# Keys' features times values in a linear-attention kernel: two heads to a product, 64 columns held and 34 moving

## The chip, the cores and the metric

The kernel runs on one core of one Trainium2 chip. The metric is the device time in microseconds of one execution. The core's engines are TensorE (PE; its weight loads are shown as PEld), VectorE (DVE), ScalarE (ACT), GpSimd (POOL) and SyncE (SP); transfers are issued from queues and run on 16 DMA engines. TensorE writes its products to PSUM, eight banks of 128 partitions x 512 fp32. A product holds one operand (the "held" columns, at most 128, loaded as weights) and streams the other (the "moving" columns, at most 512) past it. TensorE's array can be split by columns, so that several products with few held columns run side by side, each in its own tile and to its own partitions of PSUM.

## The reference

With S = 2048 rows, D = 512, H = 32 heads of 16 and F = 1792, all fp32:

```
qkv   = x @ wqkv                                  # q, k, v: 32 heads of 16 columns
phi_q = [softmax(q_h w_phi_h), softmax(-q_h w_phi_h)]     # 32 features a head
phi_k = [softmax(k_h w_phi_h), softmax(-k_h w_phi_h)]
kv_h  = phi_k_h^T v_h       (32 x 16)             # z_h = sum over rows of phi_k_h
o_h   = (phi_q_h kv_h) / (phi_q_h z_h + 1e-6)
a     = o @ wo
b     = relu(x @ w1 + b1)^2 @ w2 + b2
g     = sigmoid(sum(x * gate_w))
out   = g * a + (1 - g) * b
```

The change concerns kv_h and z_h: for every head the product of 32 features and 16 values (with a column of ones for z_h: 17), summed over all 2048 rows.

## The kernel before

**The order of the work.** The kernel doesn't issue instructions directly. A planner (class Plan) collects every operation with its reads and writes, gives each a cost (`lengths`, line 202) and a due time, and plays the engines forward. What it starts first on an engine comes first in that engine's instruction stream, so the order on every queue, the DMA issues of SP among them, is set by those costs. All instructions are issued from one line, L363, so the profile's groups are told apart by their tiles. TensorE's work is divided into groups (`nc.product()`); the planner looks at the first five groups that are left (LOOK) and takes the first that can start at the earliest time, so a group whose operands are late can be overtaken by up to four others. For a product of less than 128 x 128 held elements the planner's cost is that of line 214: at least 0.0214 us, and 0.00027 us per moving column for held blocks other than 1,024 elements.

**The stages.** Rows are taken in four blocks of 512, in two pairs r = 0, 1. A first phase makes the hidden layer x @ w1 and the queries ("u" products) and the keys' features and the values ("v" products) by a scheme with seven half-size products p1 to p7 in place of eight; each is split into a high and a low part and computed as three 128x512 products (`mm3`). Results of the hidden layer and the queries go to DRAM and come back later. A second phase, one step t for each of 4 x 14 blocks of w2, multiplies the hidden layer by w2 ("down"), and in between makes the queries' features (`do_e`, `do_phi`), the numerators (`do_n`), and the product with wo (`attend`).

**The keys' side.** The v products for one group of rows give two chunks of 128 rows: the keys' logits in banks vA and vB, the values in banks vE and vB. The steps are in `v_step`:

- p2 and p4 end the logits of the two chunks and call `features`: `exps` (largest and smallest of each head by two TENSOR_REDUCE, one subtraction of 1024 elements that writes each head twice, two exponentials on ScalarE), `sums` (sum and reciprocal) and `scaled`. The result, 32 features a head for 32 heads in the order of the heads, lies in a buffer e or ez.
- p7 and p3 put the values of the two chunks into vext[1] (an add on VectorE) and vext[0] (a copy on ScalarE). In vext each head has 17 columns, the last of which is one (set once by a memset).

`kv_burst` (line 721) then multiplies. It has 32 heads x 2 chunks = 64 fp32 products, each with 128 rows, 32 held feature columns and 17 moving value columns. Four heads go side by side into the four 32-column tiles of the array, and their results into the four groups of 32 partitions of bank kv, eight blocks of 17 columns each:

```
h = 8 * (b // 2) + 2 * a + b % 2
nc.tensor.matmul(ps[32 * a:32 * a + 32, b * VW:(b + 1) * VW], phi[:, 32 * h:32 * h + 32],
                 ve[:, h * VW:(h + 1) * VW], ...)
```

An add on VectorE takes the bank's 136 columns into kvs. There are eight bursts in a run, between 88 and 274 us; each is one group for the planner.

After the last, `kv_done` (line 735) spreads z from kvs (a copy and a transpose into zb, which lies in vext[0]) and puts the kv blocks into kvb, block by block for the numerators' product. `do_phi` on GpSimd and VectorE waits for zb, and `do_n` (32x32 tiles, 512 moving columns) for kvb and for the last of do_phi's transposes.

`exps` is used in three places: by `features` (tags e and ez), by `queries` for the first block (with a buffer passed in as `into`), and by `do_e` (tags XA...). `row()` hands out five buffers of 512 columns in turn.

Of the kernel before, what the change touches and what calls it, by code (L numbers as in the profile page):

```python
# [10 lines left out]
AF = mybir.ActivationFunctionType  # L11
ALU = mybir.AluOpType
# [5 lines left out]
P = 128  # L18
S, D, H, DH, F = 2048, 512, 32, 16, 1792
# [5 lines left out]
NG = 8  # L25
VW = DH + 1
# [349 lines left out]
def tile_gated_mix(ctx: ExitStack, tc: tile.TileContext, xT, xn, wqT, wkT, wphi, wv, wo, w1, b1, w2, b2, gw, out):  # L376
    nc = Plan(tc.nc)
# [3 lines left out]
    st, raw, held, turns = {}, {}, {}, {}  # L381
# [3 lines left out]
    def buf(tag, n=512, bufs=1, dtype=F32):  # L385

        i = turns[tag] = turns.get(tag, -1) + 1
        return View(Buffer(sbuf, shadows[n], f"{tag}_{i % bufs}", n, dtype), shadows[n])

    banks = {t: psum.tile([P, 512], F32, tag=t, name=t) for t in ("uA", "uE", "uB0", "uB1", "vA", "vB", "vE", "kv")}  # L390
# [9 lines left out]
    row = lambda: buf("row", 512, 5)  # L400
# [7 lines left out]
    def mm3(o, a, b, sa, sb, first, last):  # L408
        (ah, al), (bh, bl) = a, b
        for i, (x, y) in enumerate(((ah, bh), (ah, bl), (al, bh))):  # L410
            nc.tensor.matmul(o, x[:, sa], y[:, sb], start=first and i == 0, stop=last and i == 2, skip_group_check=True)
# [8 lines left out]
    const = lambda name, *shape: sbuf.tile([P, *shape], F32, tag=name, name=name)  # L420
# [3 lines left out]
    gate, rest = (const(n, NB * NC) for n in ("gate", "rest"))  # L424
    kvb = const("kvb", NK, 2, 2 * DH)
    tc.nc.gpsimd.memset(kvb, 0.0)
    kvs = const("kvs", NG * VW)
    tc.nc.gpsimd.memset(kvs, 0.0)
    wkept = dram.tile([NPW, 3, 2, P, 512], F32, name="wkept")
    wkept4 = dram.tile([NPW, 2, P, 256], F32, name="wkept4")  # L430
# [2 lines left out]
    vext = [const(f"vext{i}", H * VW) for i in range(2)]  # L433
    heads = lambda v: v.rearrange("p (h v) -> p h v", v=VW)
# [105 lines left out]
    def queries(b, k, src):  # L540

        t = row()
        nc.vector.transpose(t, src)
        if b == ORDER_B[0]:
            if k % 2 == 0:
                st["e0", k // 2] = buf(("tb", "phiT")[k // 2], 4 * D)
            st["e", 0, k] = sums(exps(t, into=st["e0", k // 2][:, k % 2 * 2 * D:(k % 2 + 1) * 2 * D]), f"r{k}")
        else:
            nc.sync.dma_start(qkept[b, k], t)
# [111 lines left out]
    def vproduct(ps, v, p, first, last):  # L661
        xo, ko = PAIRS[p]
        s = slice(v[1] * P, (v[1] + 1) * P)
        nc.product()
        for kk in range(2):
            mm3(ps, st["X", xo, kk], st["K", ko, kk], s, ALL, first and kk == 0, last and kk == 1)

    def exps(ps, tag="e", into=None):
        pv = ps.rearrange("p (h f) -> p h f", f=DH)
        ends = small("ends", 2 * H).rearrange("p (h t) -> p h t", t=2)  # L670
        ef = buf(tag, 2 * D, 2 if tag == "e" else 1) if into is None else into
        e = ef.rearrange("p (h t f) -> p h t f", t=2, f=DH)
        for t, op in enumerate((ALU.max, ALU.min)):
            nc.vector.tensor_reduce(ends[:, :, t], pv, AX.X, op)
        nc.vector.tensor_tensor(e, pv.unsqueeze(2).to_broadcast([P, H, 2, DH]), ends.unsqueeze(3).to_broadcast([P, H, 2, DH]),
                                ALU.subtract)
        for t, scale in enumerate((1.0, -1.0)):
            nc.scalar.activation(e[:, :, t, :], e[:, :, t, :], AF.Exp, scale=scale)
        return ef.rearrange("p (h f) -> p h f", f=DH)
# [11 lines left out]
    def features(n, ps):  # L691
        e3, r = sums(exps(ps, "ez" if n % 3 == 2 else "e"))
        st["phi", n] = scaled(e3, r)

    def v_step(v, p):
        n = 8 * v[0] + 2 * v[1]
        each = lambda x: x.rearrange("p (h f) -> p h f", f=DH)
        if p == "p1":
            vproduct(banks["vA"], v, p, True, False)
            nc.scalar.activation(banks["vB"], banks["vA"], AF.Copy)  # L700
        elif p == "p2":
            vproduct(banks["vA"], v, p, False, True)
            features(n, banks["vA"])
        elif p == "p5":
            vproduct(banks["vE"], v, p, True, False)
            st["t5", v] = slot("Vt5")
            nc.scalar.activation(st["t5", v], banks["vE"], AF.Copy)
        elif p == "p6":
            vproduct(banks["vB"], v, p, False, False)
            nc.vector.tensor_tensor(banks["vE"], banks["vB"], st["t5", v], ALU.add)  # L710
        elif p == "p7":
            vproduct(banks["vB"], v, p, False, False)
            nc.vector.tensor_tensor(heads(vext[1])[:, :, :DH], each(banks["vB"]), each(st["t5", v]), ALU.add)
        elif p == "p3":
            vproduct(banks["vE"], v, p, False, True)
            nc.scalar.activation(heads(vext[0])[:, :, :DH], each(banks["vE"]), AF.Copy)
        else:
            vproduct(banks["vB"], v, p, False, True)
            features(n + 1, banks["vB"])

    def kv_burst(v):
        n = 8 * v[0] + 2 * v[1]
        ps = banks["kv"]
        nc.product()
        for m in range(2):
            phi, ve = st["phi", n + m], vext[m]
            for b in range(NG):
                for a in range(4):
                    h = 8 * (b // 2) + 2 * a + b % 2
                    nc.tensor.matmul(ps[32 * a:32 * a + 32, b * VW:(b + 1) * VW], phi[:, 32 * h:32 * h + 32],  # L730
                                     ve[:, h * VW:(h + 1) * VW], start=(m == 0 and b == 0), stop=(m == 1),
                                     skip_group_check=True)
        nc.vector.tensor_tensor(kvs, kvs, ps[:, :NG * VW], ALU.add)

    def kv_done():
        kv = kvs.rearrange("p (b v) -> p b v", v=VW)
        z = row()[:, :NG * 32]
        nc.vector.tensor_copy(z.rearrange("p (b f) -> p b f", f=32), kv[:, :, DH].unsqueeze(2).to_broadcast([P, NG, 32]))
        nc.vector.transpose(zb, z)
        kv = kvs.rearrange("p (k u v) -> p k u v", u=2, v=VW)  # L740
        for m in range(2):
            nc.vector.tensor_copy(kvb[:, m::2, :, DH * m:DH * (m + 1)], kv[:, m::2, :, :DH])

# [50 lines left out]
    def do_e(i, k):  # L794
        t = load(slot(("XS30h", "XS30l", "XS31h", "XS31l")[k]), qkept[ORDER_B[i], k])
        n = NK * i + k
        st["e", i, k] = sums(exps(t, E_PLACES[n % 4]))
# [156 lines left out]
    def run(seq):  # L954
        for u, p in seq:
            if p == "burst":
                kv_burst(u)
            else:
                (v_step if len(u) == 3 else u_step)(u, p)
# [30 lines left out]
    vs1 = v_stream([(1, m, "kv") for m in range(NC)], (0, NC - 1, "kv"))  # L990
    run(us1[:2] + merged(us1[2:len(us1) - 5], vs1) + us1[len(us1) - 5:])
    kv_burst((1, NC - 1, "kv"))


# [4 lines left out]
    when = lambda s, f, *a: steps.setdefault(s, []).append(lambda: f(*a))  # L999
    NT = NB * NF  # L1000
    when(1, kv_done)
    when(5, wo_ready)
    for i in range(NB):
# [8 lines left out]
    for t in range(NT):  # L1012
        for f in steps.get(t, ()):
            f()
        i, f = divmod(t, NF)
# [11 lines left out]
        if last:  # L1027
            ends = [bank() for j in range(2)]
# [7 lines left out]
        for c in range(NC):  # L1036
            n = ORDER_B[i] * NC + c
# [58 lines left out]
```

## Time and profile before

| what | us |
|---|---|
| median of 3 runs | 484.05 (483.94 to 484.32) |
| the profiled execution | 484.64 |
| its span, first to last instruction | 482.8 |
| PE busy | 477.6 |
| DVE busy | 398.3 |
| ACT busy | 245.6 |
| POOL busy | 190.3 |
| DMA | 107.84 MB, mean 223 GB/s |

The span is what the engines' rows cover; the time of the execution is 1.8 us longer. A row of a group reads: line, engine, operation, output<-input, held rows*columns for TensorE, shapes, count | busy us, mean ns of one | idle us before it and who ended it. fp32 products appear as two LDWEIGHTS and two MATMUL rows each; a product on split operands (`mm3`) as one of each per part. Matmuls are pipelined: one of 512 columns lasts 0.39 us in the rows while the next starts 0.23 us after it.

### The profile page before, as it was taken

To read this page: it belongs to the slowest core of one execution; us is meant where nothing else is said; L and a number is where in the kernel's file an instruction comes from. 1 tells how busy PE (TensorE), PEld (TensorE's weight loads), DVE (VectorE), ACT (ScalarE), POOL (GpSimd) and SP (SyncE) were. 2 spreads that over 40 slices of the span, in tenths; PEclk is the share of its full clock that TensorE was granted. 3 is DMA by queue.
4 is the path that set the end of the run, shared out by engine and by line. 5 is a ranking of instruction groups with operands and counts; after the bars stand their busy time and mean duration, and the time that the engine had idled before them with its cause. 6 is when DMAs were issued, how large, how long until landed. Compare 5 with 4: busy or idle time off the path is not lost.

```text
span 482.8 us, 9455 instructions
## 1 busy us (share of the span) xinstructions
PE 477.6 (99%) x3512; PEld 384.1 (80%) x3512; DVE 398.3 (82%) x555; ACT 245.6 (51%) x439; POOL 190.3 (39%) x186
## 2 busy tenths in 40 slices
PE   9999999999999999999999999999999999999997
PEld 4878888888878888888888888788878887888785
DVE  4996898979897848999888879899999999991313
ACT  5896989642688656436688822532254205312200
POOL 1020657842663203111022489386457628740000
PEclk9999999999999999999999999999999999999999
DMA  7999867875588788855799996536612673326302
GB/s 272 365 401 335 301 236 270 298 271 175 198 261 260 256 296 284 280 197 148 260 344 329 336 368 200 181 128 207 218 57 64 193 260 115 109 88 191 93 0 87
DMA packets 61421, 107.84 MB, mean 223 GB/s; under 512 B 6848, under 2 KB 11200, under 8 KB 61376
## 3 DMA queue, kind: packets, MB, share of 16 engines
q1 hardware_dynamic: 60768, 106.33, 64.8%
q10 hardware_dynamic: 576, 0.92, 0.8%
q8 instruction: 27, 0.44, 0.4%
q14 instruction: 18, 0.15, 0.1%
q0 software_dynamic: 32, 0.01, 0.0%
HBM read 62.14 MB, written 45.09 MB: 222 GB/s over the span
## 4 chain that ended last, share of the span: by engine, by line
PE 91%; DMA 3%; DVE 3%; ACT 1%; SPq 1%; issue 0%; DVEq 0%; ACTq 0%
PE uB L363 29%; PE uA L363 16%; PE uE L363 16%; PE vB L363 10%; PE vA L363 8%; PE vE L363 7%; PE kv L363 5%; DMA KT30h<-in_w 1%; DMA wkept<-O0l 1%; DMA hkept<-b2b 1%; SPq L363 1%; DVE tb L363 0%; DVE O1l L363 0%; DVE XS11l L363 0%; DVE KT31h L363 0%
## 5 line engine op out<-in xcount | busy, mean ns | idle before, releaser
L363 POOL TENSOR_TENSOR ez<-XA,vext 128x512 f32<-128x512 f32 x24 | 34.3, 1446 | 22.3 <-DVE XS21l L363 7.3
L363 PE MATMUL uA<-XA,O0h 128*128 128x512 f32 x128 | 39.5, 390 | 0.0
L363 ACT ACTIVATE row<-row 128x512 f32<-128x512 f32 x53 | 32.2, 623 | 0.3
L363 ACT ACTIVATE XA<-XA 128x512 f32<-128x512 f32 x24 | 14.1, 630 | 34.3 <-DVE XA L363 34.2
L363 POOL TENSOR_TENSOR row<-row,wo 128x512 fp32r<-128x512 f32 x8 | 10.4, 1295 | 50.7 <-ACT wo L363 40.7
L363 PEld LDWEIGHTS uA<-XA,O0h 128*128 128x128 f32 x128 | 23.9, 188 | 5.0
L363 ACT ACTIVATE O0h<-ring 128x512 fp32r<-128x512 f32 x17 | 10.7, 628 | 31.2 <-PE uB L363 15.8
L363 PE MATMUL uA<-XA,O0l 128*128 128x512 f32 x64 | 24.9, 389 | 0.0
L363 POOL TENSOR_TENSOR row<-row,b2b 128x512 fp32r<-128x512 f32 x10 | 13.0, 1299 | 27.8 <-DMA qkept<-row 16.5
L363 DVE TENSOR_REDUCE dz<-ez 128x64 f32<-128x1024 f32 x16 | 19.3, 1205 | 2.6 <-POOL ez L363 2.6
L363 PE MATMUL uB<-XA,O3h 128*128 128x512 f32 x64 | 19.8, 391 | 0.0
L363 ACT ACTIVATE O1h<-ring 128x512 fp32r<-128x512 f32 x17 | 10.7, 630 | 14.5 <-PE uB L363 11.6
L363 DVE TENSOR_TENSOR XA<-XA,w 128x1024 f32<-128x1024 f32 x12 | 17.8, 1480 | 0.0
L363 DVE TENSOR_REDUCE sm<-e 128x64 f32<-128x1024 f32 x11 | 13.4, 1217 | 5.0 <-ACT e L363 4.9
L363 DVE RECIPROCAL r<-sm 128x64 f32<-128x64 f32 x32 | 17.1, 538 | 0.2
L363 ACT ACTIVATE row<-b2b,rest 128x512 f32<-128x512 f32 x16 | 10.8, 715 | 10.6 <-DMA out<-row 7.7
L363 POOL TENSOR_TENSOR O1l<-ring,O1h 128x512 fp32r<-128x512 f32 x9 | 13.8, 1533 | 4.8 <-ACT O1h L363 4.8
L363 ACT ACTIVATE wo<-row 128x512 fp32r<-128x512 f32 x17 | 10.6, 625 | 9.7 <-DMA hkept<-wo 8.4
L363 DVE TENSOR_TENSOR e<-e,r 128x1024 f32<-128x1024 f32 x11 | 15.0, 1374 | 0.2
L363 DVE TENSOR_TENSOR uE<-uB,ol 128x512 f32<-128x512 f32 x16 | 11.1, 692 | 4.4 <-PE uB L363 4.4
L363 ACT ACTIVATE e<-e 128x512 f32<-128x512 f32 x22 | 13.0, 622 | 3.1 <-DVE e L363 3.0
L363 DVE TENSOR_REDUCE sm<-XA 128x64 f32<-128x1024 f32 x12 | 14.3, 1202 | 0.0
(934 smaller groups left out, 1753.6 us busy)
## 6 DMA issues: line engine op xcount, KB each, us to landing
hkept<-row SPq DMA_DIRECT2D x53, 256.0 KB, 4.2
ring<-hkept SPq DMA_DIRECT2D x24, 256.0 KB, 2.7
hkept<-b2b SPq DMA_DIRECT2D x16, 256.0 KB, 3.1
hkept<-wo SPq DMA_DIRECT2D x16, 256.0 KB, 3.8
xn<-in_xn SPq DMA_DIRECT2D x16, 256.0 KB, 4.6
O0h<-hkept SPq DMA_DIRECT2D x16, 256.0 KB, 3.7
O0l<-hkept SPq DMA_DIRECT2D x16, 256.0 KB, 3.9
O1h<-hkept SPq DMA_DIRECT2D x16, 256.0 KB, 3.8
```

The lines of the kernel that those rows point to most:

```text
L363: call(*map(real, op.args), **{k: real(a) for k, a in op.kw.items()})
```

## The change

Two neighbouring heads of a burst share one product: 64 columns of features are held, and the 2 x 17 value columns of both heads move. Of the 64 x 34 result, the two diagonal 32 x 17 blocks are the heads' own, and the other two (one head's features with the other's values) are not used. A burst has 32 fp32 products in place of 64; they go into two 64-column tiles, to partitions 0 to 63 and 64 to 127.

For that the two heads have to lie side by side. The keys' features are written with the even heads first and the odd heads behind them (the subtraction of `exps` is made in two halves, only for tags e and ez without `into`), and the values are put into vext in the same order (`paired`, `paired_out`). kvs and the add behind a burst have 8 x 34 = 272 columns in place of 136. kv_done first copies the own blocks out of kvs into a row buffer, with four copies on VectorE, one for each 32 partitions, and goes on from there.

```diff
-    kvs = const("kvs", NG * VW)
+    kvs = const("kvs", NG * 2 * VW)
...
+    def paired(x, f):
+
+        return x.rearrange("p (n u f) -> p u n f", u=2, f=f)
+
...
-        nc.vector.tensor_tensor(e, pv.unsqueeze(2).to_broadcast([P, H, 2, DH]), ends.unsqueeze(3).to_broadcast([P, H, 2, DH]),
-                                ALU.subtract)
+        for u in range(2) if into is None and tag[0] == "e" else (None,):
+            o, i, n = (slice(u * H // 2, (u + 1) * H // 2), slice(u, H, 2), H // 2) if u is not None else (slice(0, H), slice(0, H), H)
+            nc.vector.tensor_tensor(e[:, o], pv[:, i].unsqueeze(2).to_broadcast([P, n, 2, DH]),
+                                    ends[:, i].unsqueeze(3).to_broadcast([P, n, 2, DH]), ALU.subtract)
...
-        each = lambda x: x.rearrange("p (h f) -> p h f", f=DH)
+        each = lambda x: paired(x, DH)
+        paired_out = lambda x: x.rearrange("p (u n v) -> p u n v", u=2, v=VW)[:, :, :, :DH]
...
-            nc.vector.tensor_tensor(heads(vext[1])[:, :, :DH], each(banks["vB"]), each(st["t5", v]), ALU.add)
+            nc.vector.tensor_tensor(paired_out(vext[1]), each(banks["vB"]), each(st["t5", v]), ALU.add)
...
-            nc.scalar.activation(heads(vext[0])[:, :, :DH], each(banks["vE"]), AF.Copy)
+            nc.scalar.activation(paired_out(vext[0]), each(banks["vE"]), AF.Copy)
...
-                for a in range(4):
-                    h = 8 * (b // 2) + 2 * a + b % 2
-                    nc.tensor.matmul(ps[32 * a:32 * a + 32, b * VW:(b + 1) * VW], phi[:, 32 * h:32 * h + 32],
-                                     ve[:, h * VW:(h + 1) * VW], start=(m == 0 and b == 0), stop=(m == 1),
+                for a in (0, 2):
+                    h = H // 2 * (b % 2) + 4 * (b // 2) + a
+                    nc.tensor.matmul(ps[32 * a:32 * a + 64, b * 2 * VW:(b + 1) * 2 * VW], phi[:, 32 * h:32 * h + 64],
+                                     ve[:, h * VW:(h + 2) * VW], start=(m == 0 and b == 0), stop=(m == 1),
...
-        nc.vector.tensor_tensor(kvs, kvs, ps[:, :NG * VW], ALU.add)
+        nc.vector.tensor_tensor(kvs, kvs, ps[:, :NG * 2 * VW], ALU.add)
 
     def kv_done():
-        kv = kvs.rearrange("p (b v) -> p b v", v=VW)
+
+        own = row()[:, :NG * VW]
+        for a in range(4):
+            rows = slice(32 * a, 32 * a + 32)
+            nc.vector.tensor_copy(own[rows].rearrange("p (b v) -> p b v", v=VW),
+                                  kvs[rows].rearrange("p (b j v) -> p b j v", j=2, v=VW)[:, :, a % 2, :])
+        kv = own.rearrange("p (b v) -> p b v", v=VW)
...
-        kv = kvs.rearrange("p (k u v) -> p k u v", u=2, v=VW)
+        kv = own.rearrange("p (k u v) -> p k u v", u=2, v=VW)
```

## The prediction

> **What bounds the kernel now.** I read the page's head first, then its chain of waits, then the stages.
>
> ```profile
> span 482.8 us, 9455 instructions
> PE 477.6 (99%) x3512; PEld 384.1 (80%) x3512; DVE 398.3 (82%) x555; ACT 245.6 (51%) x439; POOL 190.3 (39%) x186
> PEclk9999999999999999999999999999999999999999
> PE 91%; DMA 3%; DVE 3%; ACT 1%; SPq 1%; issue 0%; DVEq 0%; ACTq 0%
> ```
>
> TensorE is busy 99% of the span at full granted clock and carries 91% of the chain, so time added to or taken from its stream should move the end about one for one; 482.8 - 477.6 = 5.2 us is all the idle time there is to win back elsewhere. The columns of the next view, stages of the time in which the eight bursts run, are the stretch's length, then each engine's busy time.
>
> ```profile
> 162.00:192.00 30.00, 30.00 (x256) 24.76 (x255) 21.05 (x33) 19.75 (x37) 5.36 (x5) 1.00 0.87 290
> 192.00:222.00 30.00, 30.00 (x256) 24.76 (x255) 29.34 (x41) 11.88 (x21) 4.13 (x5) 1.00 0.63 203
> ```
>
> TensorE has no gap in either. VectorE (third) has 9 us to spare in one and 0.7 in the other: the second cover to watch.
>
> Now one burst (kv_burst, line 721), in the chain and then in the timeline:
>
> ```profile
> 86.98 1.36 PE uB L363 x6
> 88.34 1.20 PE kv L363 x82
> 89.54 1.59 PE uB L363 x6
> ...
> 88.27 1.27 PE L363 MATMUL kv<-vext,e 128*32 128x17 f32 x128
> 89.47 0.30 PEld L363 LDWEIGHTS uB<-XA,O3h 128*128 128x128 f32 x2
> ```
>
> The burst takes 1.20 us of the chain, and the product behind it 1.59 instead of 1.36, so 1.43 together and 8 x 1.43 = 11.4 us in all: the most that any version of the burst could save. The 64 products of the code are 128 matmuls, because each fp32 product is two passes, each with its own weight load.
>
> **What paces a burst.** The next view counts the burst's matmuls (second item) and loads (third item) from just before its start to four moments.
>
> ```profile
> 88.26:88.32 0.06, 0.05 (x4) 0.05 (x8) 0.00 (x0) 0.00 (x0) 1.00 1.19 444
> 88.26:88.35 0.09, 0.08 (x8) 0.08 (x12) 0.00 (x0) 0.00 (x0) 1.00 1.09 410
> 88.26:88.70 0.44, 0.43 (x50) 0.43 (x52) 0.00 (x0) 0.00 (x0) 1.00 1.01 373
> 88.26:89.20 0.94, 0.93 (x110) 0.93 (x112) 0.00 (x0) 0.00 (x0) 1.00 1.03 375
> ```
>
> From 88.70 to 89.20 come 60 matmuls, one per 8.3 ns. Four column tiles take them in turn, so a tile gets one pass per 33 ns. Two things could set that. One is the tile: at the start, where the instructions were queued up already, four loads (one per tile) came in each 0.03 us, which is about the time of a 32-column load itself. The other is the supply of instructions: a product (two loads, two matmuls) every 17 ns is also what the fold shows, in sixteen 32x32 tiles:
>
> ```profile
> 39.71 0.29 PE L363 MATMUL vB<-KT41h,KT40h 32*32 32x128 f32 x1
> ...
> 39.83 0.29 PE L363 MATMUL vA<-KT41h,KT40h 32*32 32x128 f32 x1
> ```
>
> Between these two starts lie 7 steps (vB, vE, kv, vA, vB, vE, kv, vA), so 0.12 / 7 = 17 ns each. Today supply and tile agree within what these rows resolve. The change pulls them apart: half as many products to supply, but 64 columns to load per pass and two tiles in place of four.
>
> What a 64-column load costs is not in the trace; the two ends are. Columns are min/median/max ns in the first row and busy us, mean ns in the second:
>
> ```profile
> L363 PEld LDWEIGHTS kv<-vext,e x704: 106/109/113, 88.3 to 273.4; 128*32 128x32 f32 x176
> L363 PEld LDWEIGHTS uA<-XA,O0h 128*128 128x128 f32 x128 | 23.9, 188 | 5.0
> ...
> 477.96 0.19 PEld L363 LDWEIGHTS vA<-KT40h,O0l 128*128 128x128 f32 x1
> ...
> 478.92 0.19 PEld L363 LDWEIGHTS vB<-KT41l,O1h 128*128 128x128 f32 x1
> ```
>
> From 32 to 128 columns a load grows from 106 to 188 ns, 82 / 96 = 0.85 ns per column. That makes an occupancy of 27 ns for 32 columns (the 0.03 above) and 109 for 128. The latter shows behind the burst: two loads within 0.30 us, each lasting 0.19, so the second began 0.11 after the first. For 64 columns my estimate is 55 ns. The turn of a tile is longer than its load by 33 - 27 = 6 ns in the burst and, in the last stage (eight steps from 477.96 to 478.92, 120 ns each), by 11. So a 64-column tile turns in 55 + 6 to 55 + 11, 61 to 66 ns, or 55 if nothing is added; I take 60. The moving columns hide under it, as two passes of 512 columns in one tile of the numerators' product show:
>
> ```profile
> 306.19 0.59 PE L363 MATMUL vA<-XA,kvb 32*32 32x512 f32 x1
> ...
> 306.61 0.59 PE L363 MATMUL vA<-XA,kvb 32*32 32x512 f32 x1
> 306.81 0.61 PE L363 MATMUL vB<-XA,kvb 32*32 32x512 f32 x1
> ```
>
> They are 0.42 us apart, so 34 columns take some 28 ns.
>
> **The sum, part by part.**
>
> 1. *The bursts.* Per tile 64 / 2 = 32 passes, as before 128 / 4 = 32. Each costs 60 instead of 33 ns: 32 x 27 = 0.86 us per burst, 8 x 0.86 = **+6.9 us**. With 55 it is 8 x 32 x 22 = +5.6, with 66 it is +8.4. Nothing hides it, since TensorE has no gap there.
> 2. *The product behind a burst.* It pays 1.59 - 1.36 = 0.23 us today. Part of that is the change of tile form, which stays; part is that the burst left no instructions in store, and a burst paced by its tiles would leave some. Between 0 and 8 x -0.23 = -1.8; I take **-0.2**, nearer the first, because one 109 ns load after the change of form is in it anyway.
> 3. *VectorE during the bursts.* exps subtracts in two halves for the 16 keys' features, and kvs grows to 272 elements.
>
> ```profile
> L363 DVE TENSOR_TENSOR e<-vB,ends 128x1024 f32<-128x1024 f32 x6 | 7.3, 1215 | 0.1
> L363 DVE TENSOR_TENSOR vE<-vB,Vt 128x512 f32<-128x512 f32 x8 | 5.5, 691 | 1.5 <-PE vB L363 1.5
> L363 DVE TENSOR_TENSOR kvs<-kvs,kv x8: 234/282/297, 90.5 to 273.9; 128x136 f32<-128x136 f32 x8
> ```
>
>    Two halves cost 2 x 691 - 1215 = 0.17 us more, two such splits per burst 0.33; the wider kvs add costs 136 more elements at (1215 - 691) / 512 = 1.02 ns, 0.14. That is 0.47 us of VectorE per burst against 0.86 more of TensorE: 29.34 + 0.47 still fits into 30.86. The paired order of p7's add and p3's copy moves the same 512 elements; I cost it at nothing under the same cover. But the planner (line 214) prices a small product at 0.0214 us whatever its columns, so it plans a burst 32 x 0.0214 = 0.68 us shorter, while I expect 0.86 longer. Behind each burst VectorE's written-out order then stands up to 1.5 us too early, and whatever is queued there behind an add that waits for TensorE waits with it. If that ate the cover in the tight stage, TensorE would wait up to about 1 us, once or twice: 0 to +2, I take **+0.3**, near nothing, since in the other stage 9 us are free. A re-made order may also save: at most a part of the 5.2 us of idle; I take nothing.
> 4. *kv_done.* Four copies of the own blocks come between the last kvs add and all that follows.
>
> ```profile
> 273.90 0.28 DVE L363 TENSOR_TENSOR kvs<-kvs,kv 128x136 f32<-128x136 f32 x1
> 274.21 0.29 DVE L363 COPY row<-kvs 128x256 f32<-128x256 f32 x1
> 274.42 0.29 DVE L363 COPY kvb<-kvs 128x64 f32<-128x64 f32 x2
> 275.21 3.00 POOL L363 TENSOR_TENSOR ez<-tb,vext 128x512 f32<-128x512 f32 x2 [3.53 <-DVE vext L363]
> 305.24 1.25 DVE L363 STREAM_TRANSPOSE XA<-phiT 128x1024 f32<-128x1024 f32 x1
> ...
> L428 POOL MEMSET kvs<- x1: 230/230/230, 2.2 to 2.2; 128x136 f32 x1
> ...
> POOL 1020657842663203111022489386457628740000
> ```
>
>    A copy of 136 elements lies between the 64 and the 256 of these rows; two short ones took 0.29 together, so one is 0.15 to 0.29 and four 0.6 to 1.2 us; with 0.14 for the wider add, zb is about 1 us later. GpSimd has been idle 3.53 us for zb at that point, and the chain from it ends in the transpose that lands at 306.49, in the middle of the numerators' product (do_n), which already lost 0.2 us to it (306.61 to 306.81). So this delay has little cover of its own; what hides it is that the planner may put up to four other products ahead of do_n. Between 0 and +1.2; I take **+0.3**. On VectorE the splits of the w2 and wo weights are queued behind the copies; they are due later and nothing else waits. No DMA is issued that was not before, one row slot more is turned over, and the longer memset of kvs (0.23 us today, at 2.2 us) lies in the first slice of the span, where GpSimd is a tenth busy.
>
> The Trainium skill ("VectorE: DVE Perf Modes", section "Two Vector instructions with no wait between them") has an instruction held until all earlier ones are done when it starts in another quadrant than the one before. The four copies start at partitions 0, 32, 64 and 96, so by that rule they would not overlap at all and the upper end of their bounds would hold; the sum would be 0.3 higher at most. No run here shows such copies.
>
> Sum: 6.9 - 0.2 + 0.3 + 0.3 = +7.3 us. The profiled execution took 484.64 us in all (1.8 around its span), which gives 491.9; it lies 0.6 above the median of the three, 484.05, on which I put the same +7.3: **491.3 us**.
>
> **Rivals.**
>
> *A turn costs the same whatever the columns.* Then a tile's 33 ns is a fixed price per pass, 32 passes cost 32 x 33 = 1.06 us as before, and only the +0.6 of steps 3 and 4 is left: 484.6, no change. For it: today's turn can be read as a floor. Against: loads of 32 and 128 columns differ by 82 ns. The Trainium skill ("TensorE: Matmul & The Clock Gate", section "Wait — 56ns, not 53.3ns?") has such a floor of about 25 ns between starts of small matmuls; by that figure, per tile, a burst would cost 0.80 us and the kernel would be some 2 us faster. The trace has 8.3 ns between starts, so a floor could only hold within one tile. 9%.
>
> *The supply of instructions alone paces the burst*, and it becomes faster. A product every 17 ns needs 32 x 17 = 0.54 us, 0.52 less than 1.06: 8 x -0.52 = -4.2, plus 0.6, gives 480.4. For it: the 17 ns in two quite different tile forms. Against: it decides only if a tile of 64 columns turns in 17 ns, as two tiles share the supply, and at the start of a burst, with the queue full, a tile of 32 columns took 28 to 33. 8%.
>
> *The two tiles don't run side by side* (or the form isn't taken as two tiles). 64 passes in a row at 60 ns are 3.84 us, 2.78 more than now, 8 x 2.78 = +22: 506. Against it: the four tiles of today plainly overlap. 3%.
>
> *VectorE becomes the bound behind the bursts*: the upper ends of steps 3 and 4, 2.0 + 1.2 instead of 0.6, so 491.3 + 2.6 = 493.9. For it: 29.34 of 30; against: most stages have room. 6%.
>
> **Chances and range.** The forecast has 74%. About 0.2%, 1 us, is what can be told from no change. Slower: 74 + 3 + 6 = 83%, less 1 for surprises: 82; same 9; faster 9. The forecast's own range, with 55 to 66 ns and the other bounds, is 488 to 494.5. Both rivals without a loss hold 17%, so the range reaches down to the no-change one, 484.0 to 494.5; outside are the supply rival, the tiles in a row and some 5% of the rest.
>
> **What would show it.** In the new profile the burst's matmuls read 128*64 with 34 moving, 64 to a burst, and a load lasts about 133 ns (106 + 32 x 0.85). Right: a burst's piece of the chain near 2.0 us and one matmul per 30 ns. Wrong: pieces of 1.1 (fixed turn) or 0.6 (supply). Step 4 is right if do_n starts with a wait under 0.5 us; step 3 if no gaps appear between the bursts.

## The result, and the profile after

| | before | changed |
|---|---|---|
| median, us | 484.0 (483.84 to 484.32) | 491.47 (491.12 to 492.09) |
| ratio | | 1.0152, 95% interval 1.0139 to 1.0164 |
| span of the profiled execution, us | 482.8 | 490.0 |
| TensorE instructions (MATMUL) | 3512 | 3000 |

The change removes 512 matmuls and as many weight loads, and the kernel is 7.5 us (1.5%) slower. The head of the page and the chain of waits of the changed kernel:

```profile
span 490.0 us, 8458 instructions
PE 484.5 (99%) x3000; PEld 389.8 (80%) x3000; DVE 393.6 (80%) x572; ACT 246.3 (50%) x439; POOL 197.5 (40%) x189
...
PEclk9999999999999999999999999999999999999999
...
PE 92%; DVE 3%; DMA 2%; issue 1%; ACT 1%; SPq 1%; DVEq 0%
```

TensorE still bounds it, at full granted clock, and its busy time has grown by 6.9 us, nearly all of the 7.2 that the span has. The burst that was shown of before now stands in the chain like this (start, length, engine, tile, count):

```profile
87.36 1.36 PE uB L363 x6
88.72 1.99 PE kv L363 x64
90.71 1.58 PE uB L363 x6
```

1.99 us in place of 1.20: 0.79 more, and 8 x 0.79 = 6.3 us. The product behind it takes 1.58, as it did (1.59). What is inside a burst, by tile (min/median/max ns) and by cumulative counts from just before its start (second item matmuls, third loads):

```profile
L363 PEld LDWEIGHTS kv<-vext,e x352: 132/138/139, 88.6 to 280.0; 128*64 128x64 f32 x176
L363 PE MATMUL kv<-vext,e x352: 223/224/246, 88.7 to 280.0; 128*64 128x34 f32 x176
...
88.64:89.14 0.50, 0.49 (x17) 0.49 (x18) 0.00 (x0) 0.00 (x0) 1.00 0.63 139
88.64:90.14 1.50, 1.49 (x52) 1.49 (x52) 0.00 (x0) 0.00 (x0) 1.00 0.86 281
```

By these counts 35 matmuls in 1.00 us are one per 28.6 ns. From the first of the burst's 64 matmuls to the last, 63 steps in 1.84 us, it is 29.1, so each of the two tiles turns in about 58 ns, where each of the four turned in 33. A load lasts 132 ns at the least, 26 more than one of 32 columns.

The rest of the loss shows in the numerators' first product. The first row is its first matmul, the second the first matmul of the product behind it, in the kernel before; then the same of the changed kernel, with the transpose it waits for:

```profile
305.73 0.61 PE L363 MATMUL vA<-XA,kvb 32*32 32x512 f32 x1
...
308.04 0.50 PE L363 MATMUL uA<-KT40h,O0h 128*128 128x512 f32 x1
```

```profile
314.40 0.61 PE L363 MATMUL vA<-XA,kvb 32*32 32x512 f32 x1
...
315.24 1.25 DVE L363 STREAM_TRANSPOSE XA<-phiT 128x1024 f32<-128x1024 f32 x1
...
317.57 0.50 PE L363 MATMUL uB<-KT40h,O0h 128*128 128x512 f32 x1
```

Before, it held TensorE for 308.04 - 305.73 = 2.31 us. Now it begins at 314.40, the transpose lands at 316.49, and the next product starts at 317.57: 3.17 us, 0.86 more. 6.3 + 0.86 is the whole 7.2 of the span; single waits elsewhere came and went and balance. The kernel before has one of 0.49 us at 144 that the changed one hasn't (0.72 us from one matmul's start to the next, where 0.23 is usual). One that came stands before the last burst, 0.46 us by the starts of the matmuls (0.69 from 275.91 to 276.60):

```profile
276.60 0.73 PE L363 MATMUL uB<-XA,O3h 128*128 128x512 f32 x2 [0.30 <-DVE row L363]
```

The add on VectorE that ends this wait (275.86 to 276.54) is queued behind a reduction of the keys' features, which had itself been held up 0.62 us by ScalarE.

### The profile page after: what moved, and what is told of

Same layout as the page of the kernel before. It is cut to its first block, busy times and chain, and to the rows that moved or that the text cites. A ratio compares the mean times of both kernels' runs of the same rounds, so it can differ in the third digit from the quotient of the medians.

```text
span 490.0 us, 8458 instructions
## 1 busy us (share of the span) xinstructions
PE 484.5 (99%) x3000; PEld 389.8 (80%) x3000; DVE 393.6 (80%) x572; ACT 246.3 (50%) x439; POOL 197.5 (40%) x189
## 4 chain that ended last, share of the span: by engine, by line
PE 92%; DVE 3%; DMA 2%; issue 1%; ACT 1%; SPq 1%; DVEq 0%
PE uB L363 29%; PE uE L363 16%; PE uA L363 16%; PE vB L363 10%; PE vA L363 8%; PE vE L363 7%; PE kv L363 6%; DMA KT30h<-in_w 1%; DMA wkept<-O0l 1%; SPq L363 1%; DVE ends L363 0%; DVE e L363 0%; DVE tb L363 0%; DVE O1l L363 0%; DVE row L363 0%
## 5 line engine op out<-in xcount | busy, mean ns | idle before, releaser
L363 POOL TENSOR_TENSOR ez<-XA,vext 128x512 f32<-128x512 f32 x24 | 35.3, 1492 | 14.8 <-DVE dz L363 7.6
L363 POOL TENSOR_TENSOR row<-row,wo 128x512 fp32r<-128x512 f32 x10 | 14.5, 1450 | 37.8 <-ACT wo L363 25.8
L363 ACT ACTIVATE XA<-XA 128x512 f32<-128x512 f32 x24 | 13.9, 633 | 22.5 <-DVE XA L363 22.5
L363 POOL TENSOR_TENSOR O0l<-ring,O0h 128x512 fp32r<-128x512 f32 x10 | 13.9, 1388 | 11.0 <-ACT O0h L363 11.0
L363 POOL TENSOR_TENSOR dz<-dz,r 128x64 f32<-128x64 f32 x16 | 10.2, 640 | 13.5 <-DVE r L363 9.6
L363 DVE TENSOR_TENSOR XA<-XA,w 128x1024 f32<-128x1024 f32 x12 | 15.3, 1274 | 0.0
L363 DVE TENSOR_TENSOR row<-uB,ol 128x512 f32<-128x512 f32 x17 | 11.6, 685 | 4.5 <-PE uB L363 3.6
```

The costliest lines, as they stand in the source:

```text
L363: call(*map(real, op.args), **{k: real(a) for k, a in op.kw.items()})
```

## The experiments

The theory was that the number of held columns sets the turn of a tile, because the loads pace a burst, and that the remaining microsecond comes from kv_done's copies and from the planner's price of a product. The medians of the kernel before that these runs are compared with were 484.17 to 484.3; differences from it in us are worked out from the ratios.

**34 moving, 32 held.** Only the moving side of the change, in the kernel before (vext gets 17 columns of ones behind the last head):

```diff
-ps[32 * a:32 * a + 32, b * VW:(b + 1) * VW], phi[:, 32 * h:32 * h + 32], ve[:, h * VW:(h + 1) * VW]
+ps[32 * a:32 * a + 32, b * 2 * VW:(b + 1) * 2 * VW], phi[:, 32 * h:32 * h + 32], ve[:, h * VW:(h + 2) * VW]
```

> The kernel before, with each product of a burst moving 34 value columns (its head's and the next one's) while it still holds 32; only the own 17 columns of each result are added into kvs. Theory (the columns held set the tile's turn): a burst keeps its pace of one matmul per 8.3 ns, its piece of the chain stays at 1.2 us, and the time is 484.0 to 484.5. Rival (the columns moved set it): a tile's turn goes from 33 to about 58 ns, a burst costs 0.8 us more, and the time is about 490.3.

484.18 us, ratio 0.9998 (0.9988 to 1.0009). The burst in its chain, and its matmuls:

```profile
88.16 1.24 PE kv L363 x116
89.40 1.58 PE uB L363 x6
...
L363 PE MATMUL kv<-vext,e x704: 192/197/219, 88.1 to 273.2; 128*32 128x34 f32 x176
```

Each matmul lasts 9 ns longer (192 for 183 at the least), and 128 of them take 1.24 us in place of 1.20. Twice the moving columns cost next to nothing: the second head's values are free, and the rival falls.

**64 held, 17 moving.** Only the held side, in the changed kernel:

```diff
-ps[32 * a:32 * a + 64, b * 2 * VW:(b + 1) * 2 * VW], phi[:, 32 * h:32 * h + 64], ve[:, h * VW:(h + 2) * VW]
+ps[32 * a:32 * a + 64, b * VW:(b + 1) * VW], phi[:, 32 * h:32 * h + 64], ve[:, h * VW:(h + 1) * VW]
```

> The changed kernel, with each product holding 64 feature columns but moving 17 value columns, those of the first of its two heads; kvs has 136 columns and kv_done reads it without the four copies, as before. The second head of each pair gets the first one's values, so its own block is left out. Theory (columns held): a tile's turn stays at 58.5 ns, the last matmul of a burst starts 1.84 us after the first, and the time is 8 x 0.79 = 6.3 us above before: 490.0 to 490.7. Rival (columns moved): a turn of about 33 ns, 484.0 to 484.5. Rival (supply of instructions, a product per 17 ns): about 480.

490.93 us, 1.0136 (1.0116 to 1.0155), 6.6 us above before (5.6 to 7.5).

```profile
88.12 1.98 PE kv L363 x64
90.10 1.59 PE uB L363 x6
```

The whole cost of the burst is there with half of the moving columns. The two runs together say that the held columns set the time.

**48 held, 17 moving** in the same 64-column tile. As the run before, with `phi[:, 32 * h:32 * h + 48]` to `ps[32 * a:32 * a + 48, ...]`.

> As the run with 64 held and 17 moving columns, but with 48 feature columns held in each product (half of the second head's features are left out too). If the turn of a tile grows with the columns held, it is 48 x 0.85 + 4 = 45 ns: the last matmul of a burst starts 1.41 us after the first, 8 x 0.32 = 2.6 us above before and some 0.3 for the rest, 486.5 to 488.2. If it is set by the tile's width of 64 whatever is held in it, the turn stays at 58.5 and the time at 490.5 to 491.5.

487.21 us, 1.0057 (1.0042 to 1.0072), +2.8.

```profile
L363 PEld LDWEIGHTS kv<-vext,e x352: 119/125/125, 87.5 to 275.9; 128*48 128x48 f32 x176
...
87.50:87.80 0.30, 0.29 (x13) 0.29 (x14) 0.00 (x0) 0.00 (x0) 1.00 0.20 7
87.50:88.70 1.20, 1.19 (x53) 1.20 (x54) 0.00 (x0) 0.00 (x0) 1.00 0.52 97
...
87.58 1.55 PE kv L363 x64
```

40 matmuls in 0.90 us, 22.5 ns each, make a turn of 45 ns in two tiles, as expected: not the width of the tile but the columns loaded into it count. The loads last 106, 119, 132 and 188 ns at 32, 48, 64 and 128 columns, 13 ns for each 16, or 0.81 to 0.88 ns a column. By the Trainium skill ("TensorE: Matmul & The Clock Gate", section "LDWEIGHTS (loading the stationary operand)") a load takes the number of its columns divided by 1.2 ns, whatever the rows. The trace agrees with the 0.83 ns a column of this in the differences alone: the durations are some 80 ns longer (106 ns at 32 columns, where an estimate by the page's figure is 27). The rows count for little here too: loads of 32 columns by 32 rows last 101 to 104 ns, by 128 rows 106 to 113.

**16 held, 17 moving.** Is there more to win on the other side? The kernel before, with half the features left out:

```diff
-ps[32 * a:32 * a + 32, b * VW:(b + 1) * VW], phi[:, 32 * h:32 * h + 32],
+ps[32 * a:32 * a + 16, b * VW:(b + 1) * VW], phi[:, 32 * h:32 * h + 16],
```

> The kernel before with only the first 16 of each head's 32 features held (the products for the softmax of the negated logits are left out, 64 products a burst as before). If the columns held alone set the pace, a tile's turn falls to about 14 + 4 = 18 ns and the last matmul of a burst starts 0.6 us after the first: 484 - 8 x 0.5 = 480. If the supply of instructions, a product per 17 ns, is a second bound that happens to lie at the same place, only the first 32 matmuls, which were queued up, come faster, the rest keep 8.3 ns, and the time is 483.5 to 484.3.

483.92 us, 0.9997 (0.9988 to 1.0006): nothing to win.

```profile
88.37:88.57 0.20, 0.19 (x28) 0.19 (x32) 0.00 (x0) 0.00 (x0) 1.00 0.94 338
88.37:88.77 0.40, 0.39 (x49) 0.39 (x51) 0.00 (x0) 0.00 (x0) 1.00 1.03 389
88.37:89.27 0.90, 0.89 (x109) 0.89 (x111) 0.00 (x0) 0.00 (x0) 1.00 0.99 371
```

From 88.77 to 89.27 come 60 matmuls, the same 8.3 ns each as with 32 columns. So there is a second bound that doesn't move with the columns, at two loads and two matmuls per 17 ns. The reading that fits is the supply of instructions, because only the first 33 matmuls, whose instructions could be stored up while the product before them ran, come faster: here 25 ns from one turn of a tile to the next (28 matmuls in the first 0.19 us), with 32 columns held 31.7, and behind them 33.3 in both. So 33 ns is not a fixed price of a pass, and with 32 held columns the two bounds lie nearly together, the supply a little above the loads. The 25 ns are not the 18 ns of the load either; whether a floor per tile (the Trainium skill's page above, section "Wait — 56ns, not 53.3ns?", has about 25 ns between starts of small matmuls) or the start of one instruction after the other holds them, these rows can't tell.

**The layout alone.** The changed order of features and values, with the old bursts, the old kvs and no copies:

```diff
-                for a in (0, 2):
+                for a in range(4):
...
-ps[32 * a:32 * a + 64, b * 2 * VW:(b + 1) * 2 * VW], phi[:, 32 * h:32 * h + 64], ve[:, h * VW:(h + 2) * VW]
+ps[32 * a:32 * a + 32, b * VW:(b + 1) * VW], phi[:, 32 * h:32 * h + 32], ve[:, h * VW:(h + 1) * VW]
```

> The changed layout alone: features written with even heads first in two halves, values in the same order, but bursts of 64 products with 32 columns held and 17 moving, kvs of 136 columns, kv_done without the copies. Theory: the extra VectorE work (16 x 0.17 = 2.7 us) is hidden behind TensorE, 484.0 within 0.5. Rival (VectorE bounds the tight stages): some of the 2.7 us appears, 485 to 486.7.

485.51 us, 1.0029 (1.0015 to 1.0043): +1.4 (0.7 to 2.1; the medians differ by 1.2). So the loss is the rival's in size; whether VectorE's work or the plan makes it, this run doesn't say. Which part of the layout it is was tried next.

**The layout alone, with one subtraction.** As that run, but the keys' subtraction is one instruction again, with a destination of four dimensions (`e` as "n u t f", read from a buffer in the order "u n t f").

```diff
-for u in range(2) ...: nc.vector.tensor_tensor(e[:, o], pv[:, i]..., ends[:, i]..., ALU.subtract)
+o4 = ef.rearrange("p (u n t f) -> p n u t f", u=2, t=2, f=DH)
+nc.vector.tensor_tensor(o4, i4, n4, ALU.subtract)
```

> The layout alone once more, but with the keys' subtraction as one instruction of 1024 elements that writes even heads first and odd heads behind them. If the 1.2 to 1.4 us of the layout come from the second VectorE instruction of each split (16 x 0.17 us with little cover), they go: 484.0 to 484.6. If they come from the other order of the values or of the plan, they stay: 485.0 to 486.0.

484.19 us, 1.0001 (0.9992 to 1.001): the loss is gone. The instruction by tile, split and unsplit:

```profile
L363 DVE TENSOR_TENSOR e<-vB,ends x12: 651/678/691, 77.5 to 267.5; 128x512 f32<-128x512 f32 x12
```

```profile
L363 DVE TENSOR_TENSOR e<-vB,ends x6: 1186/1221/1226, 77.4 to 265.8; 128x1024 f32<-128x1024 f32 x6
```

2 x 678 - 1221 = 0.135 us for each of the 16, 2.2 us of VectorE, of which 1.4 came through to the end, with bursts of 1.20 us. Taking it away settles that it is the split or the plan that comes with it. The plan does change: with the split GpSimd has 195 instructions and 206.6 us of work, without it 186 and 191.7, as before (186 and 190.3). Which of the two it is, and at which place the time is lost, stays open: the one profile of the split layout (a span of 483.2, from one of its faster executions) has no wait of that size.

**The copies alone.** The kernel before, with the four copies ahead of kv_done:

```diff
+        own = row()[:, :NG * VW]
+        for a in range(4):
+            rows = slice(32 * a, 32 * a + 32)
+            nc.vector.tensor_copy(own[rows]..., kvs[rows]...)
+        kv = own.rearrange("p (b v) -> p b v", v=VW)
```

> The kernel before, with the four copies of 32 partitions x 136 elements ahead of everything else in kv_done, and nothing else changed. Theory (the copies delay zb, and with it the chain that ends in the first numerators' product): that product takes up to 0.9 us longer than its 2.6 us, and the time is 484.5 to 485.0. Rival (other products go ahead of it): 484.0 within 0.3, and the 0.86 us that this product takes longer in the changed kernel comes from something else.

484.79 us, 1.0008 (0.9999 to 1.0018): +0.4, which the interval doesn't tell surely from nothing. The trace does show the delay at that place:

```profile
307.14 0.61 PE L363 MATMUL vA<-XA,kvb 32*32 32x512 f32 x1
...
310.19 0.50 PE L363 MATMUL uB<-KT40h,O0h 128*128 128x512 f32 x1
...
273.95 0.93 DVE L363 COPY row<-kvs 32x136 f32<-32x136 f32 x4
275.24 1.39 DVE L363 COPY kvb<-row 128x64 f32<-128x64 f32 x2
276.56 0.43 DVE L363 STREAM_TRANSPOSE vext<-row 128x256 f32<-128x256 f32 x1
...
275.14 1.34 POOL L363 TENSOR_TENSOR KB221l<-KT40l,KB221h 128x512 fp32r<-128x512 f32 x1 [8.31 <-ACT KB221h L363]
```

The numerators' product takes 310.19 - 307.14 = 3.05 us, 0.74 more than before (2.31, not the 2.6 that the expectation has), close to the 0.86 of the changed kernel. In the run with 64 held and 17 moving columns, which has the long bursts but not the copies, it takes 2.31 (from 312.65 to 314.96), as before. So with these plans the copies bring the delay, whether all of it reaches the end or only half.

**The planner told.** The changed kernel with one price changed:

```diff
+            if rows * cols == 64 * P:
+                return 0.25, 0.0693
             if rows * cols < P * P:
```

> The changed kernel with one number of the planner different: a product with 64 columns held costs 0.0693 us (32 of them 2.2 us, what a burst costs in the changed kernel's trace) in place of 0.0214. Theory (part of the loss beyond the bursts is a plan that takes them for 1.5 us shorter than they are): the 0.46 us wait before the last burst and some of the 0.86 us in the first numerators' product go, 490.3 to 491.0. Rival (the price only renames the order, the waits are those of the longer chain): within 0.4 of the changed kernel, 491.1 to 491.9. Under both the bursts keep their +6.3.

490.06 us, 1.0121 (1.0107 to 1.0135), 1.4 us faster than the changed kernel. Its bursts are the same; its first numerators' product isn't delayed any more, though the copies are still there, and the wait before the last burst is gone:

```profile
313.06 1.25 DVE L365 STREAM_TRANSPOSE XA<-phiT 128x1024 f32<-128x1024 f32 x1
...
313.43 0.61 PE L365 MATMUL vA<-XA,kvb 32*32 32x512 f32 x1
...
315.73 0.50 PE L365 MATMUL uB<-KT40h,O0h 128*128 128x512 f32 x1
```

2.30 us, as before the change. The copies delay zb here as much as in the changed kernel (it is ready 3.4 us after the last kvs add begins in both, 1.2 before the change), so the copies alone don't make the loss: it takes an order that doesn't put enough in front of the numerators. What is left, 5.9 us (5.2 to 6.5), is the bursts' 6.3 within its interval. So even with the planner's price mended the idea is slower than the kernel before, and no run found a version that beats that one: fewer held columns meet the supply of instructions, more held columns meet the loads.

## Why the prediction was right, point by point

- *What bounds the kernel, and what would show it.* Right: TensorE's stream was lengthened and the end moved one for one. The burst's piece of the chain came out at 1.99 (2.0 was said), the load at 132 ns (133), one matmul per 29 ns (30). The signs named for steps 3 and 4 did not hold: a gap did appear between the bursts, 0.46 us, and the numerators' product was delayed by 0.86, not by less than 0.5.
- *Step 1, the bursts, +6.9.* Measured 8 x 0.79 = 6.3. The turn of a tile is about 58 ns, a little under the 60 that was taken from the bounds 55 to 66; the mechanism, columns held, was shown by the runs with 34 moving, with 17 moving and with 48 held. Two readings behind it were not right. The 33 ns of the kernel before are the supply's for most of a burst, and the tile's own turn is the 31.7 of its start; that moves the sum by little. And the bound of 66 was taken from loads of 128 columns that come every 120 ns; their matmuls move 256 columns, and those that move 512 start 0.23 us apart, so there the columns moved set the pace and not the load:

```profile
477.96 0.28 PE L363 MATMUL vA<-KT40l,O0h 128*128 128x256 f32 x1
478.08 0.28 PE L363 MATMUL vA<-KT40h,O0l 128*128 128x256 f32 x1
```

- *Step 2, the product behind a burst, -0.2.* Nothing was saved: 1.58 against 1.59. A burst paced by its tiles didn't shorten what the product behind it pays.
- *Step 3, VectorE and the plan, +0.3.* What it feared, VectorE's written-out order standing too early, was seen once: the 0.46 us before the last burst. That the split is hidden under longer bursts is borne out loosely: the run with 64 held and 17 moving has the split, though not the wider add, and lies 0.3 above its bursts, within its interval of 0.9 to either side; with short bursts, in the layout alone, 1.4 us came through. Mending the misjudged price gained 1.4 us, more than the 0.3 allowed here and within the bound of 2, and much of it at step 4's place.
- *Step 4, kv_done, +0.3.* The place was right, the size was not: 0.86 in the changed kernel, 0.74 with the copies alone, inside the bounds of 0 to 1.2 but nearer the end that was not taken. The four copies take 0.93 us where they meet no GpSimd work, 0.22 each and one behind the other, inside the 0.6 to 1.2 that was said; but zb came 2.2 us later and not about 1 (see the last section). The step reckoned that the planner would put other products ahead; with its wrong price it did not put enough of them there, and with the right one the product lost nothing at the same delay of zb. So steps 3 and 4 were one thing in part: their +0.6 stands against about 1.2 measured.
- *The sum.* +7.3 was forecast, +7.5 came. That it is so near is luck: 0.6 too much in step 1 is made up by 0.2 that step 2 didn't save and 0.6 too little in steps 3 and 4. The range's upper end, 494.5, is not what the steps' own upper bounds add up to, 484.05 + 8.4 + 2.0 + 1.2 = 495.7; the measured time lies far below both.
- *The rivals.* A turn that costs the same whatever the columns, and a supply that alone sets the pace, are both refuted for 64 columns (0.79 us more per burst, and 45 ns at 48 columns); at 32 and 16 a bound of the supply's size is real. That the tiles don't run side by side is refuted by a matmul per 29 ns, half of a turn. VectorE as the bound behind the bursts isn't seen, but for the one wait of 0.46 us.

## What to carry to other kernels

When small products share an array in column tiles, count passes per tile and the columns loaded in each, not instructions alone: halving the products while doubling what each holds leaves the loads as many columns in all, with half as many tiles to take them side by side. Look for both bounds of such a burst, the supply of instructions and the load of a tile, before trading one for the other; here they lay nearly together, at some 8 ns a matmul, so neither fewer nor more held columns could gain, while the moving side was free. And where an order is planned from prices, a change of form needs its price changed too; here that alone was worth 1.4 us.

## What had not been expected of the hardware

A short copy on VectorE lasted as long as a GpSimd instruction that it met. In the changed kernel, the copies out of kvs by tile, then VectorE's and GpSimd's rows at that time:

```profile
L363 DVE COPY row<-kvs x4: 220/224/1333, 280.8 to 282.6; 32x136 f32<-32x136 f32 x4
...
280.77 2.04 DVE L363 COPY row<-kvs 32x136 f32<-32x136 f32 x4
...
281.19 1.29 POOL L363 TENSOR_TENSOR KB221l<-KT40l,KB221h 128x512 fp32r<-128x512 f32 x1 [0.59 <-POOL KB220l L363]
```

Three copies take 0.22 us and one 1.33, and that one lies over a GpSimd subtraction of two SBUF operands that lasts 1.29. The same subtraction met another copy of kv_done in the run with the copies alone (two copies of 64 elements in 1.39 us together, shown above, where two took 0.29 before). In the run with the planner told it met a copy of 256 elements (1.17 us, where it took 0.29 before). In the kernel before, the copies were over when GpSimd started, and this subtraction ran on VectorE behind them; in all three plans with the four copies it went to GpSimd. So in the changed kernel the copies cost kv_done about 0.9 us themselves, and one of its copies met a collision of another 1.1: zb came 2.2 us later, where step 4 had reckoned with about 1. In the run with the planner told it came as late and cost nothing, so this alone is not why step 4 was too small. The Trainium skill ("SBUF — State Buffer", section "SBUF: two separate sides") has VectorE's faster copies and GpSimd sharing a pair of ports that one of them holds for a whole instruction; these rows agree with it. That the lock is the cause was not tried by an experiment of its own.
